# Attention decode backward on one core: the special dk stores as 120 rows from partition 8 on plus 3, 3 and 2 rows, for five heads in place of six

## The chip, the core and the metric

The kernel runs on one core of a Trainium2 chip. A time is the device time of one execution in microseconds (us); the time of a kernel is the median of its runs. Lower is better. The profile is of one further execution, taken by the hardware profiler.

## The reference

There are 64 heads (2 batches of 32), one query row per head, 8192 keys and values per head, and 128 channels, all in bfloat16. Computed are the softmax attention output and the gradients for q, k and v:

```python
scores = einsum("bhqd,bhkd->bhqk", q, k) * D ** -0.5     # [2, 32, 1, 8192]
p = softmax(scores)
out = einsum("bhqk,bhkd->bhqd", p, v)
# with dout: dv = p^T dout;  dp = dout v^T
# ds = p * (dp - sum(p * dp));  dq = scale * ds k;  dk = scale * ds^T q
return out, dq, dk, dv
```

For one head, k, v, dk and dv have 2 MB each. Over 64 heads 268 MB are read and 268 MB are written.

## The kernel before

**Tiles.** One head's k is a tile of 128 partitions; partition p holds 64 keys of 128 channels, that is 16 KB that lie together in the memory too. v is laid out in the same way. Below, a "row" is one partition's 16 KB. The twelve tiles (`kvt`, `NTILE`) hold k and v of six heads. dv is written over v, and dk over k, in the same tile (L473, VectorE), and the tile is stored from there. The tile is then free for a head six further on.

**Order.** A loop over steps (L504) runs through eight steps per head. TensorE transposes the tile's chunks, makes the scores and sums up `out` and `dq`; ScalarE copies the transposed chunks; VectorE makes softmax and the outer products dv and dk. The order on every engine is fixed by `pin`. The steps of up to four heads lie over one another. The dv of head i+1 is finished four steps after the dk of head i, half a head later.

**Queues.** The loads are issued by SyncE (L112, the queue q1 of the profile), in order. A load into a tile waits until the store from that tile has landed. The stores are issued by GpSimd (L491, L102, the queue q0), in order, and each waits for its outer products. Only the last head's two stores go out on SyncE, in four pieces each. The GpSimd DMAs carry eight semaphores in turn (101 to 108 in the trace), so that each of them waits as well until the GpSimd DMA eight before it has landed.

**The special stores.** For the heads in `SPREAD` the store of dk is made by `by_rows` (L94) in several DMAs. The first, with 120 rows, has `max_dma_last_dim` set, which cuts each row into two pieces of 8 KB; the others take few rows and have no cut. Between a special store and the next plain store of dk, `turn(0)` and `turn(FIRST)` (L522 to L524) reset the queue's cursor and load five rows of 16 bytes into `parts_all`, a tile that nothing reads. At the start of the program the same reset stands ahead of a load of five rows of q (L127, L129).

```python
SPREAD = {i: ((0, 120, True), (120, 125, False), (125, 128, False)) for i in range(6, 60, 10)}
BACK = {i + 1: FIRST for i in SPREAD}
...
p0, p1, cut = step
cap = {"max_dma_last_dim": NT * D} if cut else {}
pin(store_eng.dma_start(out=dst[p0:p1], in_=src[p0:p1], **cap))
```

The special heads are 6, 16, 26, 36, 46 and 56. All other stores by GpSimd are of 128 rows without a cut.

Of the kernel before, what the change touches and what calls it, by code (L numbers as in the profile page):

```python
# [19 lines left out]
SW = 32  # L20
NTILE = 12
FIRST = 5
SPREAD = {i: ((0, 120, True), (120, 125, False), (125, 128, False)) for i in range(6, 60, 10)}
BACK = {i + 1: FIRST for i in SPREAD}


@with_exitstack
def kernel(
# [65 lines left out]
    def by_rows(dst, src, steps):  # L94

        for step in steps:
            if len(step) == 1:
                turn(*step)
                continue
# [3 lines that stand above are left out]
# [14 lines left out]
    q_rows = q.rearrange("b h s d -> (b h s) d")  # L117
    NTURN = len(BACK) + sum(len(step) == 1 and step[0] > 0 for x in SPREAD.values() for step in x)
    parts_all = const.tile([CH, NTURN, 2 * QT], BF16, name="parts_all")
# [347 lines left out]
    def outer(i, w, c, ends):  # L467
# [15 lines left out]
        if c + 1 in ends:  # L483
            at = ends.index(c + 1)
            b0, b1 = (ends[at - 1] if at else 0) * CH, (c + 1) * CH
            dst = (dv_v if w else dk_v)[i]
            if w == 0 and i in SPREAD:
                by_rows(dst, h.tile[w], SPREAD[i])
            else:
# [124 lines left out]
```

## Time and profile before

| | us |
|---|---|
| median of 3 runs | 1270.78 (1270.15 to 1271.55) |
| the profiled execution's own time | 1271.98 |
| its span, first to last instruction | 1270.2 |
| TensorE busy | 1189.1 (94%) |
| VectorE busy | 1031.2 (81%) |
| data moved by DMA | 538.53 MB, 424 GB/s over the span |
| special stores, DMAs of GpSimd | 18 of 145, at L102 |

The profile lists how long each engine was busy, how much of the span was filled by the packets of each DMA queue (as a share of 16 DMA engines), who waited for whom, and for each kind of DMA how long it took from its issue to its landing. The trace has a record of each DMA packet with its queue, start, duration and size. It does not say on which of the 16 DMA engines a packet ran.

### The profile page before, as it was taken

The numbers are of one execution on the slowest core, as the hardware profiler recorded it, in microseconds if no ns is written. First come the engines' busy times: TensorE is split into PE (matmuls) and PEld (weight loads), VectorE is DVE, ScalarE is ACT, GpSimd is POOL, SyncE is SP. The second block draws the span as 40 slices with busy tenths as digits, with TensorE's granted clock in tenths as the row PEclk, the third lists the DMA queues.
The fourth block names the chain that finished last, engine by engine and source line by source line (L and its number), as shares of the span: only waits on it lengthen the run. The fifth ranks groups of instructions, "written<-read, shape, count | busy, mean of one in ns | idle before, by whom it ended". The sixth has DMA issues, their size and how long they took to land.

```text
span 1270.2 us, 24582 instructions
## 1 busy us (share of the span) xinstructions
PE 1189.1 (94%) x10056; PEld 783.6 (62%) x10056; DVE 1031.2 (81%) x2267; ACT 556.9 (44%) x769; POOL 80.2 (6%) x151
## 2 busy tenths in 40 slices
PE   6999999999999999999999999999999999999981
PEld 4666666666666666666666666666666666666650
DVE  3888888888888888888888888888888888788873
ACT  3444444444444444444444444444444444444430
POOL 0000010000010000010000010000000000000000
PEclk9999999999999999999999999999999999999995
DMA  9999999999999999999999999999999999999997
GB/s 391 419 429 429 428 430 429 429 428 429 431 427 428 429 429 430 428 429 410 431 428 430 429 428 417 425 429 429 428 430 426 429 428 430 429 429 428 429 429 317
DMA packets 39805, 538.53 MB, mean 424 GB/s; under 512 B 5180, under 2 KB 5180, under 8 KB 6460
## 3 DMA queue, kind: packets, MB, share of 16 engines
q1 hardware_dynamic: 20172, 272.70, 50.4%
q0 software_dynamic: 19520, 264.25, 49.1%
q8 instruction: 79, 1.29, 0.4%
q14 instruction: 34, 0.28, 0.1%
HBM read 268.47 MB, written 268.47 MB: 423 GB/s over the span
## 4 chain that ended last, share of the span: by engine, by line
PE 63%; DVE 14%; DMA 11%; another core or an unknown queue 6%; issue 3%; ACT 0%; SPq 0%; POOL 0%; ACTq 0%; DVEq 0%; POOLq 0%
PE tp L237 27%; PE acc L418 15%; PE raw L258 10%; DMA kvt<-in_v_dram 7%; DVE kvt L473 6%; PE sw L278 4%; DMA out_dram<-kvt 4%; DVE sel L441 3%; DVE rows L271 3%; PE sw L364 2%; PE sw L219 2%; PE sw L302 1%; DVE sel L435 1%; PE acc L455 1%
## 5 line engine op out<-in xcount | busy, mean ns | idle before, releaser
L239 ACT COPY ev<-tp 128x1024 f32<-128x1024 f32 x512 | 518.4, 1013 | 663.4 <-PE tp L237 658.0
L473 DVE TENSOR_TENSOR kvt<-qb,pair 128x2048 bf16<-128x2048 bf16 x512 | 617.2, 1216 | 0.1
L237 PE MATMUL tp<-ident_f,kvt 128*128 128x128 f32 x4096 | 547.8, 277 | 5.3 <-DMA kvt<-in_v_dram 4.6
L237 PEld LDWEIGHTS tp<-ident_f,kvt 128*128 128x128 f32 x4096 | 454.0, 144 | 86.8 <-issue 66.3
L258 PE MATMUL raw<-ev,qwin 128*32 128x512 bf16 x2048 | 209.8, 400 | 0.0
L418 PE MATMUL acc<-kvt,dS_pad 128*64 128x512 bf16 x1024 | 160.7, 395 | 0.4 <-DVE dS_pad L404 0.4
L418 PE MATMUL acc<-kvt,E_pad 128*64 128x512 bf16 x1024 | 160.2, 393 | 0.6 <-DVE E_pad L329 0.6
L278 PEld LDWEIGHTS sw<-sel,rows 128*128 128x128 f32 x1024 | 123.9, 191 | 52.4 <-DVE sel L441 25.9
L441 DVE SCALAR_TENSOR_TENSOR sel<-acc,diag,sel 128x128 f32<-128x128 f32 x384 | 134.7, 351 | 13.6
L258 PEld LDWEIGHTS <-qwin 128*32 128x32 bf16 x2048 | 52.7, 93 | 135.4 <-issue 131.0
L278 PE MATMUL sw<-sel,rows 128*128 128x16 f32 x1024 | 136.3, 265 | 0.0
L491 POOL DMA_DIRECT2D out_dram<-kvt x120 | 64.2, 535 | 1060.8 <-DVE qb L228 449.1
L271 DVE COPY rows<-raw 128x512 f32<-128x512 f32 x128 | 88.5, 692 | 49.4 <-PE raw L258 49.4
L297 DVE TENSOR_REDUCE st<-sw 1x1 f32<-1x128 f32 x64 | 17.8, 279 | 55.9 <-PE sw L296 55.9
L219 PE MATMUL sw<-ident_f,qT 128*128 128x128 bf16 x128 | 28.9, 226 | 36.3 <-DVE st L292 36.3
L418 PEld LDWEIGHTS <-dS_pad 128*64 128x64 bf16 x1024 | 36.6, 108 | 34.7 <-issue 31.5
L364 PEld LDWEIGHTS sw<-st,ones 128*128 128x128 f32 x256 | 38.2, 188 | 30.8 <-issue 15.3
L418 PEld LDWEIGHTS <-E_pad 128*64 128x64 bf16 x1024 | 36.1, 108 | 33.6 <-issue 31.5
L364 PE MATMUL sw<-st,ones 128*128 128x1 f32 x256 | 49.1, 261 | 0.0
L435 DVE TENSOR_SCALAR sel<-acc,diag 128x128 f32<-128x128 f32 x128 | 43.7, 342 | 0.0
L455 PEld LDWEIGHTS acc<-ones,sel 128*128 128x128 f32 x256 | 39.1, 193 | 7.2 <-DVE sel L441 7.2
L228 DVE CAST qb<-sw 128x128 bf16<-128x128 f32 x128 | 36.5, 285 | 7.3 <-PE sw L219 7.3
(54 smaller groups left out, 381.5 us busy)
## 6 DMA issues: line engine op xcount, KB each, us to landing
out_dram<-kvt POOLq DMA_DIRECT2D x120, 2048.0 KB, 47.6
kvt<-in_v_dram SPq DMA_DIRECT2D x64, 2048.0 KB, 18.6
kvt<-in_k_dram SPq DMA_DIRECT2D x63, 2048.0 KB, 19.6
out_dram<-kvt POOLq DMA_DIRECT2D x6, 1920.0 KB, 53.6
out_dram<-kvt SPq DMA_DIRECT2D x8, 512.0 KB, 21.5
kvt<-in_k_dram SPq DMA_DIRECT2D x2, 512.0 KB, 4.4
kvt<-in_k_dram SPq DMA_DIRECT2D x1, 1024.0 KB, 7.2
out_dram<-kvt POOLq DMA_DIRECT2D x6, 80.0 KB, 53.3
```

The costliest lines, as they stand in the source:

```text
L219: nc.tensor.matmul(h.qbp, lhsT=qT[:, w, i : i + 1].to_broadcast([P, P]), rhs=ident_bf, start=True, stop=True,)
L237: pin(nc.tensor.transpose(tp[:, m, :], two, ident_f[:]))
L239: pin(nc.scalar.copy(out=ev[:], in_=tp[:]))
L258: nc.tensor.matmul(h.raw[g * SW : (g + 1) * SW, :], lhsT=qwin[:, w, e, q0 : q0 + SW], rhs=cols[:, b, :, e], start=(c == 0), stop=(c == NCH ...
L271: pin(nc.vector.tensor_copy(out=h.rows[:], in_=h.raw[:]))
L278: nc.tensor.matmul(h.score[w].rearrange("p (n m t) -> p n m t", m=QT, t=2)[:, :, m, :], lhsT=h.rows[:, m * P : (m + 1) * P], rhs=sel4[:].r ...
L364: nc.tensor.matmul(out, lhsT=ones[:].to_broadcast([P, P]), rhs=col, start=True, stop=True)
L418: nc.tensor.matmul(h.acc[w][g : g + CW, :], lhsT=wts[:, n0 : n0 + CW], rhs=rows[:, n0 : n0 + QT, :].rearrange("p n d -> p (n d)"), start=( ...
L435: nc.vector.tensor_scalar(out=h.sel[:], in0=block, scalar1=diag[:, 0:1], scalar2=None, op0=ALU.mult)
L441: nc.vector.scalar_tensor_tensor(out=h.sel[:], in0=block, scalar=diag[:, b : b + 1], in1=h.sel[:], op0=ALU.mult, op1=ALU.add,)
L473: nc.vector.tensor_tensor(out=h.tile[w][:, n0 : n0 + CH, :].rearrange("p n (e t) -> p n e t", t=2), in0=h.qb[w][:] .rearrange("p (e t) -> ...
L491: pin(eng.dma_start(out=dst[:, b0:b1, :], in_=h.tile[w][:, b0:b1, :]))
```

## The change

The special stores take five heads, 6, 17, 28, 39 and 50, in place of six. Each stores the partitions 8 to 127 in the cut DMA of 120 rows, and then the partitions 0 to 2, 3 to 5 and 6 to 7 in three uncut DMAs, in place of the partitions 0 to 119, 120 to 124 and 125 to 127. `BACK` follows `SPREAD`, so there are five resets with their small loads, too. On GpSimd that makes 147 DMAs in place of 145: 121 plain stores (120 before), 20 parts of special stores (18), 5 small loads (6) and the one at the start. The instructions of the other engines stand as they stood.

```diff
-SPREAD = {i: ((0, 120, True), (120, 125, False), (125, 128, False)) for i in range(6, 60, 10)}
+SPREAD = {
+    i: ((8, 128, True), (0, 3, False), (3, 6, False), (6, 8, False)) for i in range(6, 56, 11)
+}
 BACK = {i + 1: FIRST for i in SPREAD}
```

## The prediction

> **What bounds the kernel now.** I read the page's DMA part first, because its row by slices is full from start to end.
>
> ```profile
> DMA  9999999999999999999999999999999999999997
> GB/s 391 419 429 429 428 430 429 429 428 429 431 427 428 429 429 430 428 429 410 431 428 430 429 428 417 425 429 429 428 430 426 429 428 430 429 429 428 429 429 317
> ...
> q1 hardware_dynamic: 20172, 272.70, 50.4%
> q0 software_dynamic: 19520, 264.25, 49.1%
> q8 instruction: 79, 1.29, 0.4%
> q14 instruction: 34, 0.28, 0.1%
> ```
>
> The shares add up to 100.0% of sixteen engines' span: loads (q1) and stores (q0) fill the DMA engines. One head moves 8.39 MB, at 429 GB/s 19.55 us. The compute is a little faster: in the chain the outer products come every 19.01 us.
>
> ```profile
> 153.89 1.22 DVE kvt L473
> 172.89 1.22 DVE kvt L473
> 191.91 1.22 DVE kvt L473
> ```
>
> So finished stores pile up: the view of line 102 has the special stores land after 23.8 us at the least (the first) and 69.9 us at the most (the last), and SyncE spends the span waiting for them.
>
> ```profile
> DMA to landing us min/median/max: 23.8/53.2/69.9
> ```
>
> The next line is from the waits of SyncE's own queue: in total, how often, the longest.
>
> ```profile
> SPq L112 <- DMA out_dram<-kvt: 1129.4, 120, 27.8
> ```
>
> With every engine always supplied, the end is set by the engine with the most work. The packet records name no engine, but a packet starts 3 to 4 ns before the one ahead of it on its engine ends, and each DMA gives an engine a known series of sizes; with these I strung the 39,805 packets into sixteen chains. From 12 us on no chain has a gap over 0.3 us before 1253 us; there one of the group of eleven runs dry for 13 us and only then gets its last small packets (the 1266.7 below). The special stores sort the chains; one row is 16 KB:
>
> ```
> group     engines  store rows                    last packet ends, us
> eleven      11     1008 = 126*8                  1268.6 1267.3 1266.7 1266.4 1265.3 1264.6 1263.8 1263.6 1263.1 1260.0 1255.3
> e3           1     1008+6  (a row of the 5)      1268.5
> e4           1     1008-48+6 (none of the 120)   1257.4
> e0 to e2     3     1008+12 (a row of 5 and of 3) 1264.6 1259.1 1258.2
> ```
>
> The cut store of 120 rows gives eight rows to fifteen engines and none to e4. A plain packet of 16 KB takes 611 ns in nearly every record (607 from start to start), but e4's stores take 635 and its loads 620 on the mean: it is the slow engine, and the specials relieve it. The five uncut rows go to e0 to e4, e4 included, and the three rows again to e0 to e2: the few-row stores begin at the same engine each time. The five are the same that get the 16-byte rows after a reset. Nine of the eleven end after 1263 us, eight of them fetching instructions in 9 or 10 packets of about 0.95 us (q8).
>
> **The change, engine by engine.** The sums are for the profiled execution: its span of 1270.2 us ends 1.6 after the last packet, and its own time of 1271.98 is 1.20 over the median of 1270.78. I take the change of the last packet over to the median.
>
> *The eleven.* 121 plain stores and five shares of eight rows are 126*8 = 1008 rows again: no change. One special fewer turns sixteen 8 KB packets into eight of 16 KB per engine: 8*(2*305-607) = 24 ns, nothing. The first stays at 1268.6.
>
> *e3* loses its six rows, as no small store has over three: 6*0.607 = 3.6, so 1268.5 becomes 1264.9.
>
> *e2* has 5*2 = 10 extra rows for 12: -1.2. *e0 and e1* have 5*3 = 15 for 12: +1.8. The latest of the three may be any of them, so at most 1264.6+1.8 = 1266.4.
>
> *e4* is spared 5*8 = 40 rows in place of 48-6 = 42: 2*0.63 = +1.3, so 1258.7. Between specials it falls behind by 16*(635-615)+16*(620-612) = 0.45 us per head. Eleven heads make 4.9 us for eight rows (5.0); ten heads made 4.5 for seven (4.4). Both keep pace, and thirteen heads without relief at the end are in the sum of rows already. The rows add up: -6-2+3+3+2 = 0.
>
> The last packet therefore stays at 1268.6 in this execution. In others the long packets (some 0.45 us over, 2 to 23 per engine) fall elsewhere, and e3 would be last in about half of them; without it the next of the eleven, 1267.3, ends up to 1.3 earlier. I take -0.3: 1270.78-0.3 = 1270.5.
>
> *GpSimd's issues.* Two DMAs more, each 507 to 765 ns on line 102, with POOL busy 6% of the span: hidden by the 9 us between stores. But DMA n waits for the landing of n-8, and a special with the dv store and small load behind it now takes six of the eight places, not five. These are the waits after the fifth special (head 46):
>
> ```profile
> 922.18 1.29 POOL L102 DMA_DIRECT2D out_dram<-kvt  x2 [9.47 <-DVE kvt L473]
> 924.50 0.51 POOL L102 DMA_DIRECT2D out_dram<-kvt  x1 [1.02 <-DMA out_dram<-kvt]
> ...
> 974.80 0.53 POOL L491 DMA_DIRECT2D out_dram<-kvt  x1 [9.20 <-DVE oT L458]
> 989.20 1.60 POOL L491 DMA_DIRECT2D out_dram<-kvt  x3 [13.87 <-DVE rows L271]
> ```
>
> The 120 rows landed at 988.7, and the fourth plain 2 MB store after the dv store waited for that until 989.2. Now the third does: issued at 989 in place of 974.8, 14 us late, with the next ones behind it. Who is hurt? The fastest engine had worked off its earlier stores at 989.1 and would stand dry for a us or two; the slowest finished them at 1014.8 and has 25 us of stock. The fastest end up to 13 us ahead of the last. So I cost this at nothing; the cover is that stock, and without it a late special costs 14.0-9.7 (a store's usual distance) = 4.3 us. SyncE's load into the special tile now waits for four landings; in the last special the small ones landed within 1.0 us of the large one, while a load takes 18.6 us to land and the next is already queued: nothing.
>
> *A rule against this.* The small stores' rows stack on the first engines: in the trace the five and the three share e0 to e2. The Trainium skill, "DMA: Bandwidth & Descriptors", section "Why a DMA increments its semaphore by 16 and not by 1", has a DMA of k rows on GpSimd's queue take k consecutive engines from a cursor that moves on. By that, 3, 3 and 2 rows would lie on the eight engines that 5 and 3 lay on, e4 among them, and e4 would be spared 35 rows only, +4.4 us, to 1261.8: still not last. The trace agrees for the 120 rows and the small load, and disagrees for the uncut ones.
>
> **The rivals.** *The spared engine moves (slower).* If partition 8, and not the queue's cursor, decides who gets none of the 120 rows, e4 gets its 42 rows back: 42*0.63 = +26, e4 ends at 1283.9, and the time is 1270.78+15.3 = 1286. Against it: the small stores from partition 120, and the small load to partition 0, begin at the same engine, so the partition does not count there.
>
> *GpSimd's wait is exposed (slower).* It decides from the point where more than the fastest engines run dry, that is where an engine loses more than its lead on the last (13.3 us at most, 1 to 5 for most). The specials of heads 39 and 50 are the late ones; one exposed gives 1270.8+4.3 = 1275.1, both 1279.4. For it: the fastest engine's stock was just used up at 989. Against it: the last engine's was not, and the three stores after the wait go out together.
>
> *e3 was the real bound (faster).* If in most runs e3 is last and the eleven's 1268.6 and 1267.3 are chance, the end falls to 1266.4 (the next of the eleven, and the bound of e0 and e1) or to 1265.3: -2.2 to -3.3, the middle 1268.0. Against it: five of the eleven end at 1264.6 or later, the one that ran dry not counted, and their rows do not change.
>
> **How the numbers follow.** A measurement of this kernel can tell about 0.2%, 2.5 us, from no change. The forecast, the same last engine, has 0.62: 1268.4 to 1272.8, from -1.3 for e3 and the runs' own spread. The exposed wait has 0.16, the moved engine 0.05; a part of e3 beyond the 2.5 us, or fewer long packets, has 0.14, and 0.03 stays for an unseen slower case. With 1275.2 as the upper end the single exposed wait is inside, with 1267.5 most of the faster case; 0.8 lies between. Same 0.62, slower 0.24, faster 0.14.
>
> **What would show it.** The after-profile's queue shares should still add up to 100%; the chains should have an engine without 8 KB packets in the specials and slow packets on it, rows as 1008, 1008, 968, 1018 and 1023, e3 no longer near the end, and the last of the eleven within 1.5 us of 1268.6. The specials' landings should be near the old course, and GpSimd's long wait should come one plain store earlier. I am wrong if e0 or e1 end last, if an engine has gaps and then ends last, or if the slow engine has 8 KB packets.

## The result, and the profile after

| | before | after |
|---|---|---|
| median, us | 1271.20 (1269.88 to 1275.06, 18 runs) | 1268.37 (1266.49 to 1269.87, 18 runs) |
| ratio to before | | 0.9975, 95% interval [0.9968, 0.9982] |
| span of the profiled execution, us | 1270.2 | 1266.1 |
| its own time, us | 1271.98 | 1267.85 |

The changed kernel is 2.8 us faster by the medians (0.22%; 0.25% by the ratio), a little more than the 2.5 us that the prediction took as the least that can be told from no change. The prediction was 1270.5, no change; 1268.4 is inside its range, at the very edge of its main case (1268.4 to 1272.8), and close to the outcome of the rival "e3 was the real bound" (1268.0).

The page's DMA part of the changed kernel, the answer to the first lines shown of before:

```profile
DMA  9999999999999999999999999999999999999998
GB/s 393 422 429 429 429 428 429 429 429 429 430 429 428 429 429 429 429 429 429 423 428 430 430 429 428 428 427 430 429 430 428 429 429 427 429 429 429 429 430 336
...
q1 hardware_dynamic: 20172, 272.70, 50.6%
q0 software_dynamic: 19456, 264.25, 49.1%
```

The same bytes, still full from start to end. Two things differ. Before had slices of 410 and 417 GB/s near its third and fourth special store; the lowest inner slice now is 422. And the last slice moves 336 GB/s in place of 317: the engines end closer together. The same in the windows of the two traces, here at the tail (columns: window, its length, busy time of PE, PEld, DVE, ACT, POOL, then PEclk, DMA share, GB/s). Before:

```profile
1250.00:1258.00 8.00, 0.00 (x0) 0.00 (x0) 0.19 (x2) 0.00 (x0) 0.00 (x0) 0.50 0.95 396
1262.00:1269.00 7.00, 0.00 (x0) 0.00 (x0) 0.00 (x0) 0.00 (x0) 0.00 (x0) 0.50 0.33 129
```

After:

```profile
1250.00:1258.00 8.00, 0.00 (x0) 0.00 (x0) 0.00 (x0) 0.00 (x0) 0.00 (x0) 0.50 0.82 342
1262.00:1265.00 3.00, 0.00 (x0) 0.00 (x0) 0.00 (x0) 0.00 (x0) 0.00 (x0) 0.50 0.18 64
```

After 1262 us before still has 0.33*16*7 = 37 us of engine work to do, after 0.18*16*3 = 9. Nothing computes there; only the packets count.

The compute's rhythm is unchanged. In the chain of waits of the changed kernel the outer products still come every 19.0 us (L473 of before is now L475):

```profile
153.33 1.22 DVE kvt L475
172.33 1.22 DVE kvt L475
191.35 1.22 DVE kvt L475
```

SyncE's waits and the specials' landing (the view of L104, L102 of before) keep their course too: 1124.7 us in 119 waits against 1129.4 in 120, and a middle landing 4 us shorter.

```profile
SPq L114 <- DMA out_dram<-kvt: 1124.7, 119, 27.5
```

```profile
DMA to landing us min/median/max: 23.3/49.2/65.3
```

The packets of the changed kernel, strung into chains in the same way:

```
group     engines  store rows  last packet ends, us
eleven      11     1008        1263.8 (ran dry for 11 us; one packet of q14), 1263.1 to 1261.6 (eight, all fetching), 1252.0, 1251.7
e3           1     1008        1263.2
e4           1     968         1259.3
e0 to e2     3     1023 1023 1018   1264.5 1259.4 (e0, e1)  1256.8 (e2)
```

The last packet is one of e0 and e1's, at 1264.5, 4.1 us before the old end of 1268.6; the span fell by the same 4.1. The 1263.8 is a single 8 KB packet of q14, no load or store of the kernel, and so is the 1266.7 in the prediction's table (it starts at 1266.1 and takes 0.56 us).

### The profile page after: what moved, and what is told of

Same layout as the page of the kernel before. It is cut to its first block, busy times and chain, and to the rows that moved or that the text cites. A ratio compares the mean times of both kernels' runs of the same rounds, so it can differ in the third digit from the quotient of the medians.

```text
span 1266.1 us, 24581 instructions
## 1 busy us (share of the span) xinstructions
PE 1187.7 (94%) x10056; PEld 783.1 (62%) x10056; DVE 1031.3 (81%) x2267; ACT 557.2 (44%) x769; POOL 80.6 (6%) x153
## 3 DMA queue, kind: packets, MB, share of 16 engines
q0 software_dynamic: 19456, 264.25, 49.1%
## 4 chain that ended last, share of the span: by engine, by line
PE 68%; DVE 16%; DMA 7%; another core or an unknown queue 4%; issue 2%; ACT 0%; SPq 0%; POOL 0%; ACTq 0%; DVEq 0%
PE tp L239 29%; PE acc L420 17%; PE raw L260 11%; DVE kvt L475 6%; PE sw L280 4%; DMA out_dram<-kvt 4%; DVE sel L443 4%; DVE rows L273 3%; DMA kvt<-in_v_dram 3%; PE sw L366 3%; PE sw L221 2%; PE sw L304 1%; DVE sel L437 1%; PE acc L457 1%
## 5 line engine op out<-in xcount | busy, mean ns | idle before, releaser
L475 DVE TENSOR_TENSOR kvt<-qb,pair 128x2048 bf16<-128x2048 bf16 x512 | 617.2, 1216 | 0.2
L457 PE MATMUL acc<-ones,sel 128*128 128x1 f32 x256 | 36.7, 212 | 6.1 <-DVE sel L443 6.1
## 6 DMA issues: line engine op xcount, KB each, us to landing
out_dram<-kvt POOLq DMA_DIRECT2D x10, 48.0 KB, 49.1
```

The costliest lines, as they stand in the source:

```text
L457: nc.tensor.matmul(h.acc[w][:, 0:1], lhsT=h.sel[:], rhs=ones[:], start=True, stop=True)
L475: nc.vector.tensor_tensor(out=h.tile[w][:, n0 : n0 + CH, :].rearrange("p n (e t) -> p n e t", t=2), in0=h.qb[w][:] .rearrange("p (e t) -> ...
```

## The experiments

The theory after the result: e3 was the usual last engine and its six rows were what counted. The rivals: what is gained is fewer long packets beside the special stores, or only the sixth special. All kernels start from before; a "long packet" took over 150 ns more than its usual 611, 309 or 159, and "excess" is what all long packets among the loads and stores of a profile took beyond that after its first 12 us. It is 92.7 us before (216 packets) and 55.8 after (143). "Far" is the part that lies apart from the code fetches: 39.6 before, 17.4 after. The edits change `SPREAD` alone; e4_none changes one more line, shown there, and the last run is the changed kernel itself.

**The parts one by one.** Rows and heads changed separately, in five kernels.

```diff
# e1_heads
-SPREAD = {i: ((0, 120, True), (120, 125, False), (125, 128, False)) for i in range(6, 60, 10)}
+SPREAD = {i: ((0, 120, True), (120, 125, False), (125, 128, False)) for i in range(6, 56, 11)}
```

> Only the heads of the special stores change: five (6, 17, 28, 39, 50) in place of six; the rows stay 0 to 119, 120 to 124, 125 to 127. Theory R (rows: the end is that of the engine with most rows, at the packet times of before): e4 is spared 35 rows in place of 42, +4.4 us to 1261.8, still not last; e3 has one row less; so 1270.6 to 1271.2, ratio 0.9995 to 1.000. Theory L (long packets: packets around the specials take longer, 92.7 us over all sixteen engines before and 55.8 after, and the number or the places of the specials decide how many): 1268.4 to 1269.2, ratio about 0.998, with under 65 us of excess in the packet records.

```diff
# e2_from8
-SPREAD = {i: ((0, 120, True), (120, 125, False), (125, 128, False)) for i in range(6, 60, 10)}
+SPREAD = {i: ((8, 128, True), (0, 5, False), (5, 8, False)) for i in range(6, 60, 10)}
```

> Only the partitions change: the 120 rows from partition 8 on, and the small stores as partitions 0 to 4 and 5 to 7; six specials at the old heads. R: every engine has the rows of before, so 1271.2, ratio 1.000. L, if the partitions that an engine reads in a special decide: most of the gain, 1268.4 to 1269.2, ratio about 0.998, excess under 65 us. If L holds by the number of specials: 1271.2 and about 90 us.

```diff
# e3_split
-SPREAD = {i: ((0, 120, True), (120, 125, False), (125, 128, False)) for i in range(6, 60, 10)}
+SPREAD = {i: ((0, 120, True), (120, 123, False), (123, 126, False), (126, 128, False)) for i in range(6, 60, 10)}
```

> Only the cut of the last eight rows changes: 120 to 122, 123 to 125, 126 and 127; six specials at the old heads, 120 rows from partition 0. R: e3 loses its 6 rows (1268.5 to 1264.9), e4 is spared 48 rows in place of 42 (1257.4 to 1253.6), e0 and e1 get 6 rows more each (1264.6 to at most 1268.2): 1270.0 to 1270.9, ratio 0.999 to 1.000; if e3 was the real bound of most runs, 1268.5 to 1269.5, ratio about 0.998. L: no change beyond 0.5 us, 1270.7 to 1271.7, unless the small stores make the long packets.

```diff
# e5_heads_split
-SPREAD = {i: ((0, 120, True), (120, 125, False), (125, 128, False)) for i in range(6, 60, 10)}
+SPREAD = {i: ((0, 120, True), (120, 123, False), (123, 126, False), (126, 128, False)) for i in range(6, 56, 11)}
```

> Two of the three parts of the change: the five heads 6, 17, 28, 39, 50, and the small stores as 3, 3 and 2 rows, but still 120 rows from partition 0 and the small ones from partition 120 on. Theory E (e3 is the bound: it loses its rows, the place in the partitions does not count): as the whole change, 1268.0 to 1268.9. Theory P (the start at partition 8 is needed): between 1268.9 and 1270.5, the time of the heads alone.

```diff
# e6_heads_from8
-SPREAD = {i: ((0, 120, True), (120, 125, False), (125, 128, False)) for i in range(6, 60, 10)}
+SPREAD = {i: ((8, 128, True), (0, 5, False), (5, 8, False)) for i in range(6, 56, 11)}
```

> The other two parts: the five heads, and 120 rows from partition 8 on, but the eight rows left as 5 and 3, so that e3 keeps one row per special (5 rows). E: as the heads alone, 1270.0 to 1271.0. P: near 1268.4 to 1269.2.

Measured, us; the ratio is to before on the same chip, the last columns are from the one profile:

```
kernel          heads rows       median  (range)              ratio  95%               last engine      e3 (extra rows) excess
before          six   0-119,5,3  1271.20 (1269.88 - 1275.06)                           eleven 1268.6    1268.5 (6)      92.7
e1_heads        five  0-119,5,3  1270.48 (1269.25 - 1271.07)  0.9988 [0.9978, 0.9998]  e3               1267.7 (5)      86.0
e2_from8        six   8-127,5,3  1273.04 (1271.15 - 1278.69)  1.0015 [1.0001, 1.0029]  e3               1269.8 (6)      68.8
e3_split        six   0-119,3,3,2 1275.74 (1270.44 - 1278.72) 1.0030 [1.0014, 1.0045]  e0 or e1 1269.8  1263.8 (0)      76.8
e5_heads_split  five  0-119,3,3,2 1272.54 (1268.23 - 1277.22) 1.0005 [0.9993, 1.0018]  e0 or e1 1269.2  1265.2 (0)      82.5
e6_heads_from8  five  8-127,5,3  1272.89 (1270.48 - 1274.98)  1.0002 [0.9990, 1.0014]  e3               1271.0 (5)      90.5
after           five  8-127,3,3,2 1268.37 (1266.49 - 1269.87) 0.9975 [0.9968, 0.9982]  e0 or e1 1264.5  1263.2 (0)      55.8
```

Three things follow. First, *e3 ends late when it has rows of the small stores*: with five or six rows more it ended at 1267.7 to 1271.0 in all four profiles and ended last in three of them, 1.2 to 4.3 us after the next group's latest; without them at 1263.2 to 1265.2. The eight fetching engines, whose rows no kernel changes, ended at 1261.0 to 1266.5 in the six profiles other than before's. Second, *the relief of e3 is not enough by itself*. In e3_split the rows went to e0 and e1, which have 6*3 = 18 extra there, and one of them is last. With fifteen, in e5_heads_split, one is last again, with 17 long packets of 7.1 us in all on it, where the changed kernel has 11 of 2.9 us. Third, the parts do not add: against the before of their own chip the heads alone are worth -0.7 us, the start at partition 8 alone +1.9, the split alone +4.6; all three together -2.8.

**Is it e4 that the specials serve?** No specials and no resets at all. The second line only keeps `parts_all` from having no slot.

```diff
# e4_none
-SPREAD = {i: ((0, 120, True), (120, 125, False), (125, 128, False)) for i in range(6, 60, 10)}
+SPREAD = {}
...
-    NTURN = len(BACK) + sum(len(step) == 1 and step[0] > 0 for x in SPREAD.values() for step in x)
+    NTURN = 1 + len(BACK) + sum(len(step) == 1 and step[0] > 0 for x in SPREAD.values() for step in x)
```

> No special stores at all (and no resets after them): 126 plain stores by GpSimd. R: the slow engine e4 gets its 42 rows back, 42 times 0.63 = 26 us, and ends at 1283.6: 1286, ratio 1.012. L says the same of the time; the packet records tell the source: if the specials make the long packets, the excess that is not beside an instruction fetch falls from 39.6 us to under 15; if not, it stays near 40.

Measured: 1285.04 (1284.41 to 1285.76), ratio 1.0105 [1.0087, 1.0124]. The windows of this kernel's trace:

```profile
1267.00:1274.00 7.00, 0.90 (x3) 0.63 (x3) 2.12 (x8) 0.00 (x0) 0.00 (x0) 0.50 0.45 181
1275.00:1280.00 5.00, 0.00 (x0) 0.00 (x0) 0.00 (x0) 0.00 (x0) 0.00 (x0) 0.50 0.06 26
```

A DMA share of 0.06 is one engine in sixteen: it works alone until 1280.6, while the others are done at 1274.2 or before. Its last nine packets of 16 KB took 614 to 631 ns, where 611 is usual. That is the slow engine, and 1285.0 is close to what the prediction gave for its relief lost (1286). The excess is only 51.4 us here, of it 8.5 far from the fetches: most of the far ones go with the special stores and their resets, which this run does not tell apart, and long packets on the other engines were not the bound here.

**A known load put back on e3.** The changed kernel with its eight small rows as 4 and 4, so that e0 to e3 get two rows each per special.

```diff
# e9_fourfour
-SPREAD = {i: ((0, 120, True), (120, 125, False), (125, 128, False)) for i in range(6, 60, 10)}
+SPREAD = {i: ((8, 128, True), (0, 4, False), (4, 8, False)) for i in range(6, 56, 11)}
```

> The changed kernel with its eight rows as 4 and 4 in place of 3, 3 and 2: e0 to e3 get two rows per special each, so e3 has 10 rows more than in the changed kernel, e2 the same, e0 and e1 5 fewer. Theory E (e3 carries work of its own, and is last as soon as it gets extra rows): 1263.2 + 10 times 0.607 = 1269.3 for e3 in place of 1264.5 for the last of the changed kernel, so 1268.4 + 4.8 = 1273.2. If rows count the same on all engines and the instruction fetches bound the kernel: 1267.0 to 1268.4.

Measured: 1278.91 (1277.75 to 1281.41), ratio 1.0064 [1.0052, 1.0076]: 10.5 us above the changed kernel, twice what was expected (1273.2). Per special, e0 and e1 have one row fewer and e3 two more, and there is one DMA fewer; nothing else differs. The windows of its trace:

```profile
1250.00:1266.00 16.00, 3.41 (x18) 1.43 (x14) 9.17 (x18) 0.00 (x0) 0.00 (x0) 0.61 0.83 337
1267.00:1278.00 11.00, 0.00 (x0) 0.00 (x0) 0.00 (x0) 0.00 (x0) 0.00 (x0) 0.50 0.07 27
```

One engine alone is busy for the last 11 us (0.07, again one in sixteen); the rest end by 1266.4. It is e3: its chain has 1018 rows, no code fetch, and the 5.9 us of q14's packets that e3 has in every profile (below). Its end, 1278.0, is 14.8 us after that of the changed kernel's e3 (1263.2). The ten rows are 6.1 us of that; long packets are most of the rest: 35 of them with an excess of 16.4 us, against 20 with 8.3 in the changed kernel. So rows on e3 cost here more than twice their own time. Many of the added ones lie at 623 to 631, 833 to 861 and 1049 to 1054 us, where the third to fifth specials are worked off; why they fall on e3 is open. The excess of this profile is the largest, 101.5 us; it is that of the slowest of the five runs, but all five took 1277.75 us or more.

**Other heads, and fewer.** The rows of the changed kernel at other heads, six to ten later, and at four heads only.

```diff
# e7_late
-SPREAD = {i: ((0, 120, True), (120, 125, False), (125, 128, False)) for i in range(6, 60, 10)}
+SPREAD = {i: ((8, 128, True), (0, 3, False), (3, 6, False), (6, 8, False)) for i in range(16, 60, 10)}
```

> The changed kernel's stores (120 rows from partition 8 on, 3, 3 and 2 rows), five specials too, but at the heads 16, 26, 36, 46 and 56. Every engine has the rows that it has in the changed kernel. E by rows alone: 1268.0 to 1268.9. Theory S (a special at head 56, 100 us ahead of the end, costs waits and long packets that nothing makes good, and makes the wide spread of the two kernels with only the partitions or only the cut changed): 1270 to 1275, with a spread of over 4 us.

```diff
# e8_four
-SPREAD = {i: ((0, 120, True), (120, 125, False), (125, 128, False)) for i in range(6, 60, 10)}
+SPREAD = {i: ((8, 128, True), (0, 3, False), (3, 6, False), (6, 8, False)) for i in range(6, 50, 13)}
```

> The changed kernel's stores at four heads (6, 19, 32, 45) in place of five. By rows from the changed kernel's packet records: e4 gets 8 rows back, 1259.3 + 5.0 = 1264.3; e0 and e1 lose 3, 1264.5 - 1.8 = 1262.7 at the latest; e3 stays at 1263.2, the eleven at 1263.1. E: the last packet ends at 1264.3 in place of 1264.5, so the same time, 1267.7 to 1268.8; if e0 and e1 are later in most runs than in the profile, 1267.0 to 1267.7.

Measured for e7_late: 1270.29 (1266.98 to 1275.46), ratio 0.9990 [0.9978, 1.0003]. Its profile, from a run near the low end, ends at 1264.4 with e3 at 1263.3. The same rows at other heads thus reach the same best times and miss them more often.

Measured for e8_four: 1267.58 (1267.16 to 1268.31), ratio 0.9967 [0.9955, 0.9979]: faster than before. Against the changed kernel the intervals overlap, and no difference is shown. The row sum carried over: e4, spared 8 rows fewer, ended at 1263.6 (1264.3 expected), e0 and e1 at 1261.1 (at most 1262.7), e3 at 1262.7, the fetching engines at 1263.4 or before. These groups now end within 2.5 us of one another, so a fifth special is not needed; by the row sum one fewer would put e4 last (1263.6 + 5.0 = 1268.6).

**The large share without the small stores.** Which of the two makes the runs spread?

```diff
# e10_from0_alone
-SPREAD = {i: ((0, 120, True), (120, 125, False), (125, 128, False)) for i in range(6, 60, 10)}
+SPREAD = {i: ((0, 120, True),) for i in range(6, 56, 11)}
# e11_from8_alone
+SPREAD = {i: ((8, 128, True),) for i in range(6, 56, 11)}
```

> Five specials at the heads of the changed kernel with the 120 rows from partition 0 alone; the small stores are left out, so that the last eight rows of dk of five heads are not written. Every engine has 1008 rows or fewer. E: the eleven and e3 are last at 1263.1 and 1263.2 in place of 1264.5: 1267.0, give or take 0.6. Theory P1 (the 120 rows from partition 0 make the long packets and the wide spread): 1268.5 to 1272, spread over 5 us. Theory P2 (the small stores from the partitions 120 to 127 make them): 1267.0, spread under 3 us.

> As the run with the 120 rows from partition 0 alone, but from partition 8; the first eight rows of dk of five heads are not written. E, P1 and P2: 1267.0, spread under 3 us. Any difference between the two is due to the partitions of the 120 rows.

Measured: e10_from0_alone 1268.64 (1267.98 to 1270.04), ratio 0.9973 [0.9960, 0.9986]; e11_from8_alone 1272.56 (1268.47 to 1280.31), ratio 1.0019 [1.0005, 1.0033]. The first agrees with the theory in part: with no row on e3 it ended at 1263.6, the fetching engines at 1264.9 or before, and the gain is that of the changed kernel; but the time is 1 us above the range expected. The second was a miss (1267.0 expected, with a spread under 3 us). The start at partition 8 is not quieter by itself; its spread of 12 us is the widest of all, and there are no small stores to blame. Its profile, from the second fastest run, ends at 1265.2 with e3 at 1263.0, so it does not show what made the others slow: a kernel without rows on e3 can be slower than before.

**Once more.** The changed kernel as it is, on the chip of the last runs.

> The changed kernel once more, on the chip of these runs: 1268.4, ratio 0.9968 to 0.9982, if the gain is not one chip's.

Measured: 1268.24 (1266.58 to 1270.82), ratio 0.9977 [0.9968, 0.9985]. The gain comes again; the last engine of this profile was one of e0 and e1 at 1266.1, with e3 at 1262.8.

## Why the prediction was right and wrong

**Right: the rows.** The chains have 1008, 1008, 968, 1018 and 1023 rows, as summed up. e4 ended at 1259.3 (1258.7 forecast), and its row sum came near in e8_four (1263.6 for 1264.3) and in e4_none (1280.6 for 1283.6). e0 and e1 ended at 1264.5, under the 1266.4 given as the most. The small stores still begin at e0 each time, from partition 0 as from 120. The spared engine did not move: that rival is out. So is a cursor that moves on with the uncut few-row stores: it would give e4 973 rows; the chain has 968. The Trainium skill's "DMA: Bandwidth & Descriptors" (section "Why a DMA increments its semaphore by 16 and not by 1"), which the prediction read this way, names an exception in the same place: some direct copies on GpSimd's queue are spread over all 16 engines, with the partitions divided by 16 and rounded up on each. That is one row each on the first engines, which agrees with the 1023, 1023 and 1018 rows on e0 to e2 and the 1008 on e3.

**Right: GpSimd's wait, and its price.** The timeline of GpSimd in the changed kernel around its last special (start, duration; in brackets the idle time before it and what ended it):

```profile
997.61 1.29 POOL L104 DMA_DIRECT2D out_dram<-kvt  x2 [9.47 <-DVE kvt L475]
999.37 0.51 POOL L104 DMA_DIRECT2D out_dram<-kvt  x1 [0.47 <-DMA out_dram<-kvt]
1009.10 0.51 POOL L104 DMA_DIRECT2D out_dram<-kvt  x1 [9.22 <-DMA out_dram<-kvt]
1019.09 0.55 POOL L493 DMA_DIRECT2D out_dram<-kvt  x1 [9.49 <-DVE sel L443]
1028.58 0.64 POOL L92 DMA_DIRECT2D parts_all<-in_q_dram  x1 [8.94 <-DMA out_dram<-kvt]
1041.37 0.56 POOL L493 DMA_DIRECT2D out_dram<-kvt  x1 [12.15 <-DVE st L386]
1048.81 0.53 POOL L493 DMA_DIRECT2D out_dram<-kvt  x1 [6.89 <-DVE st L294]
1062.77 0.53 POOL L493 DMA_DIRECT2D out_dram<-kvt  x1 [13.43 <-DVE kvt L475]
1064.21 1.60 POOL L493 DMA_DIRECT2D out_dram<-kvt  x3 [0.91 <-DMA out_dram<-kvt]
```

The 120 rows, issued at 997.61, landed at 1062.2. The third store after the dv store (1019.09) went out at 1062.77, after 13.43 us of idle time, and three more right behind it: one store earlier than before, as forecast. The bracket names VectorE, one of whose products ended at about the same time; but the store comes 0.6 us after the landing that its semaphore stands for, as the next does 0.5 us after its own (1063.7). The last small store (1009.10) and the dv store also waited, for landings at 1008.8 and 1018.5, which the prediction had not listed. Over the whole span the waits for landings that the view names for GpSimd's stores are 49.1 us in sum, 53.4 before, with a longest of 12.3 in place of 9.7 (total, times, longest; first before, then after). Waits put down to VectorE, as the 13.43 above, are not among them.

```profile
POOL out_dram L491 <- DMA out_dram<-kvt: 45.1, 5, 9.7
POOL out_dram L102 <- DMA out_dram<-kvt: 8.3, 2, 7.3
```

```profile
POOL out_dram L493 <- DMA out_dram<-kvt: 36.1, 4, 12.3
POOL out_dram L104 <- DMA out_dram<-kvt: 13.0, 3, 9.2
```

In the changed kernel's chains (after and e12_again) no DMA engine stands dry for over 1.4 us before the tail. The price of nothing held, and the rival that it is exposed is out.

**Wrong: "The last packet therefore stays at 1268.6", and -0.3 for e3.** This step failed, though the time lies in the stated range: the argument gave no change, and 1268.4 is inside because the lower end had been set to take in most of the faster case. That is luck, and one of the prediction's own signs of being wrong came: one of e0 and e1 ended last. The last of the eleven, too, was not within 1.5 us of 1268.6.

The prediction took the 1268.6 and 1267.3 of the eleven as what their rows cost, and put e3's relief at what the next of them leaves. But with unchanged rows the eight fetching engines ended at 1263.1 or before in the changed kernel, and by 1266.5 in every other profile but before's and e4_none's. The old 1268.6 held long packets of that one execution: its chain has 19 with an excess of 9.6 us, and seven of them, 4.9 us, lie at 583 to 585 and 781 to 785 us. There, at the third and fourth specials, before has 33 of its far ones (560 to 600 us) and 23 (760 to 800), and the page's row of GB/s shows its 410 and 417.

e3, by contrast, carries a constant load of its own: its chain has 5.6 to 6.0 us of the queue q14's packets in every profile (after the first 12 us), and long packets. These tend to grow with its extra rows:

```
extra rows on e3                                        long packets  excess, us
none (e4_none, after, e3_split, e5, e8, e10, e11, e12)  19 to 24      7.7 to 10.0
five or six (before, e1, e2, e6)                        23 to 27      9.8 to 12.9
ten (e9)                                                35            16.4
```

Its relief was mis-sized as well: the forecast 1264.9 counted six rows, 3.6 us; it ended at 1263.2, because its long packets fell from 9.9 to 8.3 us too. With the rows it was last in three profiles of four; without them the end can fall until e0 and e1 (1264.5) and the fetching engines (1263.1) set it. So the mis-sized term is the end that is left without e3: -0.3 was put down where the median moved by -2.8. The rival named this, but its 0.14 was too low. Its argument against, "five of the eleven end at 1264.6 or later", rested on one execution.

That e3 alone makes the gain is not shown. The kernels that gained over 0.2% (after, e12_again, e8_four, e10_from0_alone) all have e3 relieved and no more than 15 rows added on e0 and e1. But so have e5_heads_split and e11_from8_alone, which are no faster than before, and e7_late, whose interval reaches 1; e3_split has e3 relieved and is slower.

**Not forecast: fewer long packets.** The excess fell from 92.7 to 55.8 us. The prediction had them only as chance. How much of the 2.8 us is theirs is not separated. In the two profiles both had to fall for the end to fall: e3 by 5.3 us, and the latest of the fetching engines by 5.5, from 1268.6 to 1263.1 with the same rows. The whole set of stores goes with a small excess: after, e12_again, e8_four and e7_late have 54.6 to 65.9 us, all other kernels with specials 68.8 or more. This rival to e3 is open. Against it as the only cause, e10_from0_alone has 81.0 and is as fast as the changed kernel. The sum over all engines does not order the times: e2_from8 has 68.8 and is slower than before.

**Open.** Why the middle and the spread of the runs depend on the combination of start partition, cut and heads: the parts do not add, and e5_heads_split, e7_late and e11_from8_alone have spreads of 8.5 to 12 us that no row sum explains. A profile shows one execution, and several were taken in the lower part of their kernel's runs (e3_split, e7_late, e11_from8_alone), so the slower runs of these kernels were not seen from inside.

## What to carry to other kernels

Where the DMA share is full to the end, sort the work by engine: with the total unchanged, a few rows taken off the engine that ends last are worth at least their time until the next one is last, and rows on the wrong one can cost more than their time (ten on e3, 6.1 us, 10.5 us in e9_fourfour). Before pricing a relief against the next engine in one trace, ask which of the late ends come from rows or fixed loads, which return in every run, and which from long packets, some of which do not. A single small packet after a pause may not be the kernel's at all. A part of a change that loses alone can belong to a version that wins, so the whole is to be run as well.

## What the runs showed of the hardware

- Stores of 2, 3 or 5 whole rows of 16 KB from GpSimd's queue give their rows to the same engines from e0 on, whatever the partition: in the changed kernel 1023, 1023 and 1018 rows on e0 to e2 and 1008 on e3. The cut store of 120 rows left out the slow engine from partition 8 as from 0 (968 rows).
- One engine takes 635 ns for a 16 KB store and 620 for a load, where the others take 611. Without relief it costs the kernel 13.9 us (e4_none 1285.04, before 1271.13 on the same chip).
- Long packets go with the special stores and their resets: 8.5 us of excess far from the fetches without them, 39.6 with six, 17.4 with the five of the changed kernel. An excess of 597 ns comes nine times in before and thirteen times in e6_heads_from8, near the 607 of one whole 16 KB packet; that the engine there waits out a packet of another engine is argued only.
- The packets of q14 load one engine (e3) with 5.6 to 6.0 us although it fetches no code, and one of e0 and e1 with about 3.1 us.
- Rows added to e3 cost more than their own time: ten rows are 6.1 us, and its end moved by 14.8 (e9_fourfour against the changed kernel).
